# Attention and Fourier mixing on one core: sequence matrices first, one of them by two levels of seven products, the output projection in two parts

## The chip, the core and the metric

The program runs on one core of a Trainium2 chip. The metric is the device time of one execution in microseconds (us); lower is better. The time before is the median of three runs. An engine name stands for one of the core's engines: PE is TensorE (matrix products; PEld is its weight load), DVE is VectorE, ACT is ScalarE, POOL is GpSimd, and SP is SyncE, which here only issues DMA transfers.

## The reference

Two independent blocks on inputs of 2048 rows and 1024 columns; their results stand side by side in the output (2048 x 2048).

```python
# A: softmax attention with 32 heads of 32
q, k, v = split_heads(x @ wqkv)                       # 1024 x 3072
p = softmax(einsum("bhqd,bhkd->bhqk", q, k) * Dh**-0.5)
a = concat_heads(einsum("bhqk,bhkd->bhqd", p, v)) @ wo
# B: real part of a two-dimensional Fourier transform by matrices
re = einsum("bsd,ed->bse", x, dft_hid_re)             # 1024 x 1024
im = einsum("bsd,ed->bse", x, dft_hid_im)
b = einsum("ts,bse->bte", dft_seq_re, re) - einsum("ts,bse->bte", dft_seq_im, im)
out = concatenate([a, b], axis=-1)
```

## The kernel before

**Products.** Every large product runs in single precision as three passes. `halves` splits each operand into a rounded high half `hi` (a cast, on DVE or ACT) and the rest `lo` (a subtraction of two SBUF tiles, on POOL or DVE), and `group` adds hi·hi, lo·hi and hi·lo into one PSUM bank. One such pass is one PE instruction: a stationary tile of 128x128 and a moving tile of 128x512. The text calls it a *fill*, since these instructions fill the gaps that attention leaves on PE. `piece` makes a stationary operand ("h" and "l" tiles, from rings of four), `moving` makes a moving one (a numbered "slot" that holds both halves). `fetch` loads the one or two terms of an operand (tiles "raw" and "g") and adds or subtracts them on POOL or DVE.

**Seven products for eight.** Each matrix product is cut into two by two blocks and done with seven block products (`ORDER` = 1, 2, 5, 6, 7, 3, 4). Operands are sums of blocks, some reused through DRAM (`s_d`, `t_d`), and `gather` combines the results, one DVE instruction that reads PSUM ("evacuation") per group, sometimes with a further addition on POOL or DVE.

**Stages.** `qkv` makes queries, keys and values (2016 fills). `dense1` multiplies x by the two hidden matrices (7 block products x 8 row tiles x 2 matrices x 4 chunks x 3 passes = 1344 fills) and stores the results (`ab_d`). `dense2` does the two sequence matrices one after the other (2 x 7 x 8 x 8 x 3 = 2688 fills) and adds them through `y_d`. `project` multiplies the attention output, read back from `o_d`, by `wo` (7 x 8 x 4 x 3 = 672 fills). In sum 6720.

**Attention.** Per head, 64 score products and 64 transposed score products of 128x512, and 16 times four products with the values; DVE takes row maxima, ACT the exponentials. The streams S, T and V hold these.

**Order.** Nothing is scheduled at run time. `Plan` walks through the program when it is built, keeps a clock with a fixed cost for each operation, and writes one order for each engine; on the chip every engine works through its own order and waits on semaphores. The fills are one list, in the order of the code. Between them the loop puts attention so that the share of fills done keeps pace with the share of attention done (`nf / (FILL - RES) <= done / ATT`); what is then left of the list runs after the last head. `Plan` does not let POOL start while a DVE instruction that uses both SBUF ports (`two=True`) runs, nor the other way round (`choose`). It counts a DMA by its size alone, at `KB_US` = 360 KB per us.

Of the kernel before, what the change touches and what calls it, by code (L numbers as in the profile page):

```python
# [8 lines left out]
F32 = mybir.dt.float32  # L9
F32R = mybir.dt.float32r  # L10
AF = mybir.ActivationFunctionType
ALU = mybir.AluOpType
# [208 lines left out]
def kernel(  # L221
# [26 lines left out]
    ab_d = [[[dram.tile([P, NB], F32, name=f"ab_d{m}_{e}_{k}") for k in range(NS)] for e in range(2)] for m in range(2)]  # L248

    s1_d = [[dram.tile([P, 4, P], F32, name=f"s1_d{x}_{i}") for i in range(8)] for x in (5, 6)]  # L250
    t1_d = [[dram.tile([P, NB], F32, name=f"t1_d{x}_{n}") for n in range(8)] for x in (5, 6)]
# [5 lines left out]
    u3_d = [[dram.tile([P, NB], F32, name=f"u3_d{i}_{m}") for m in range(2)] for i in range(8)]  # L257
    s2_d = [[[dram.tile([P, 4, P], F32, name=f"s2_d{x}_{i}_{k}") for k in range(4)] for i in range(8)] for x in (5, 6)]
    t2_d = [[[dram.tile([P, NB], F32, name=f"t2_d{x}_{m}_{k}") for k in range(8)] for m in range(2)] for x in (5, 6)]
    y_d = [[dram.tile([P, NB], F32, name=f"y_d{i}_{e}") for e in range(2)] for i in range(NS)]  # L260
# [83 lines left out]

    MM, PV, SWITCH, TINY = 0.2275, 0.853, 0.40, 0.17
# [8 lines left out]
    RES = 400  # L354
# [7 lines left out]
    FILL = 3 * (7 * 24 * 4 + 7 * 16 * 4 + 7 * 8 * 16 + 2 * 8 * 4)  # L362
# [251 lines left out]
    def qkv():  # L614
# [216 lines left out]
        def qk_group(x, W, b, n, order=None):  # L831
# [3 lines left out]
            if p == 1 and n == 0:  # L835
                if early:
                    X[2 * b], X[2 * b + 1] = acc(b)
                else:
# [3 lines left out]
                  gather(p, 2 * b + n, qk_result(b + 8 * h[0], 2 * h[1] + n, early) if h else None, early, None if b % 2 else SCALE), order)  # L842

# [7 lines left out]
        for x, (p, blocks, v) in enumerate(STEPS[:10]):  # L851
            spare[0] = x < 5
# [69 lines left out]
    ORDER = (1, 2, 5, 6, 7, 3, 4)  # L922

# [7 lines left out]
    def gather(what, X, Y, u3, to, wrote, part=None, split=False):  # L931
# [14 lines left out]
        def finish(ps, last):  # L946
# [48 lines left out]

            if what == 1:
                return to_acc(X, None, True)
# [12 lines left out]
            if what in (2, 3):  # L1010
                return put(X.at, [X.users], X.last, ALU.add, to, wrote, part)
            if Y is None:
                return put(lambda: got["c"], [cusers], cload, ALU.subtract, to, wrote, part)
            return put(Y.at, [Y.users], Y.last, ALU.subtract, to, wrote, part)
# [3 lines left out]
    ab_st = [[[[] for _ in range(NS)] for _ in range(2)] for _ in range(2)]  # L1018

    def dense1():  # L1020
        s1, t1 = ({5: [[] for _ in range(8)], 6: [[] for _ in range(8)]} for _ in range(2))
        u3 = [[[], []] for _ in range(8)]

        def a_terms(p, i):
            q = lambda r, k: xb[8 * r + i, :, 4 * k : 4 * k + 4, :]
            return {
                1: [(1, q(0, 0), [])], 2: [(1, q(0, 1), [])], 4: [(1, q(1, 1), [])],
                5: [(1, q(1, 0), []), (1, q(1, 1), [])],
                6: [(1, s1_d[0][i], s1[5][i]), (-1, q(0, 0), [])],
                7: [(1, q(0, 0), []), (-1, q(1, 0), [])],  # L1030
                3: [(1, q(0, 1), []), (-1, s1_d[1][i], s1[6][i])],
            }[p]

        def b_terms(p, n):
            m, c = divmod(n, 4)
            q = lambda k, e: wd[m, 4 * k + c, :, e * NB : e * NB + NB]
            return {
                1: [(1, q(0, 0), [])], 2: [(1, q(1, 0), [])], 3: [(1, q(1, 1), [])],
                5: [(1, q(0, 1), []), (-1, q(0, 0), [])],
                6: [(1, q(1, 1), []), (-1, t1_d[0][n], t1[5][n])],  # L1040
                7: [(1, q(1, 1), []), (-1, q(0, 1), [])],
                4: [(1, t1_d[1][n], t1[6][n]), (-1, q(1, 0), [])],
            }[p]

        def load_b(x, n):
            p = ORDER[x]
            B[x][n] = moving((8 * x + n) % 12, b_terms(p, n), (t1_d[p - 5][n], t1[p][n]) if p in (5, 6) else None)

# [542 lines left out]
```

## Time and profile before

| What | Value |
|---|---|
| Median of 3 runs | 2942.08 us (2942.07 to 2944.09) |
| Span of the profiled execution | 2940.5 us (1.6 us under the median; the page gives no time of its own around the span) |
| PE busy, instructions | 2934.3 us (100%), 14920 |
| DVE, ACT, POOL busy | 79%, 77%, 28% |
| Granted PE clock | 1.000 |
| DMA | 562.78 MB, 191 GB/s over the span, 58.8% of 16 engines on the SP queue |

Fills run alone at first; the first score products stand at 69 us, from about 240 us attention and fills share PE, and the last products with the values end at about 2760 us, after which fills run alone again. The windows view splits the span into stretches and gives for each the busy time and the number of instructions of each engine, the mean share of the 16 DMA engines that was busy, and the rate.

### The profile page before, as it was taken

Reading aid. Unit: us, or ns where it says so; the run is one execution under the profiler, and the core shown is the slowest. Engines: PE = TensorE matmul, PEld = TensorE weight load, DVE = VectorE, ACT = ScalarE, POOL = GpSimd, SP = SyncE. Lnnn points to the kernel's source line nnn. Section 1 sums busy time; section 2 is a strip of 40 time slices with the busy share of each in tenths; the row PEclk is TensorE's granted clock in tenths of the full one; section 3 lists DMA queues with packets and bytes.
Section 4 is the critical chain, followed back from the end, with each engine's and each line's share of the span. In section 5 each row is a group of like instructions: output and inputs, shape, how many; then the busy total and the mean of one; then the engine's idle time right before and its main releaser. Section 6 shows DMA issues by size and latency. Waiting matters only on the chain.

```text
span 2940.5 us, 45511 instructions
## 1 busy us (share of the span) xinstructions
PE 2934.3 (100%) x14920; PEld 2146.0 (73%) x14920; DVE 2328.2 (79%) x3196; ACT 2278.3 (77%) x4317; POOL 833.3 (28%) x650
## 2 busy tenths in 40 slices
PE   9999999999999999999999999999999999999999
PEld 8887777777777767777777777777777777677787
DVE  7679888788877987777777898888777888887585
ACT  5347888888888888888888888888888888887431
POOL 2324335132212332241111332333112333343042
PEclk9999999999999999999999999999999999999999
DMA  9965668676525653664425775554334677555663
GB/s 372 348 229 194 195 191 292 194 251 225 191 93 164 226 189 111 205 206 147 150 84 161 237 224 189 171 167 151 110 110 139 220 238 222 168 178 176 211 209 118
DMA packets 378455, 562.78 MB, mean 191 GB/s; under 512 B 111183, under 2 KB 111439, under 8 KB 378095
## 3 DMA queue, kind: packets, MB, share of 16 engines
q1 hardware_dynamic: 378076, 559.75, 58.8%
q8 instruction: 120, 1.97, 0.3%
q14 instruction: 115, 0.93, 0.1%
q10 hardware_dynamic: 144, 0.13, 0.0%
HBM read 385.65 MB, written 174.08 MB: 190 GB/s over the span
## 4 chain that ended last, share of the span: by engine, by line
PE 98%; DMA 1%; DVE 1%; ACT 0%; issue 0%; POOL 0%; SPq 0%; DVEq 0%; POOLq 0%; ACTq 0%
PE pd L404 44%; PE psT L1400 16%; PE psS L1278 16%; PE pd L1419 15%; PE psT L404 7%; DVE negm L1284 0%; DMA raw<-in_xb 0%; DMA g<-in_ct 0%; DMA raw<-ab_d 0%; ACT psS L1287 0%; DMA g<-in_xb 0%; DMA slot<-in_xw 0%; DVE l L494 0%; POOL raw L469 0%; DVE raw L469 0%
## 5 line engine op out<-in xcount | busy, mean ns | idle before, releaser
L1404 ACT ACTIVATE pt<-psT 128x512 f32<-128x512 f32 x2048 | 1193.8, 671 | 347.3 <-PE psT L1400 345.5
L1284 DVE TENSOR_REDUCE negm<-psS 128x1 f32<-128x1024 f32 x1024 | 1241.2, 1220 | 211.5 <-PE psS L1278 204.4
L1287 ACT ACTIVATE psS<-psS,negm 128x1024 f32<-128x1024 f32 x1024 | 1188.9, 1161 | 70.9 <-DVE negm L1284 66.8
L404 PE MATMUL pd<-slot,h 128*128 128x512 f32 x3400 | 1155.7, 389 | 0.0
L1400 PE MATMUL psT<-qs,ks 128*128 128x512 f32 x2048 | 802.3, 395 | 0.0
L404 PEld LDWEIGHTS pd<-slot,h 128*128 128x128 f32 x3400 | 638.3, 188 | 132.6
L404 PE MATMUL pd<-slot,l 128*128 128x512 f32 x1700 | 661.3, 389 | 0.0
L1400 PEld LDWEIGHTS psT<-qs,ks 128*128 128x128 f32 x2048 | 381.4, 188 | 157.3 <-issue 63.7
L1278 PE MATMUL psS<-ks,qs 128*128 128x512 f32 x1552 | 472.1, 390 | 0.7 <-ACT psS L1287 0.6
L1419 PE MATMUL pd<-pt,vt 128*32 128x512 f32 x4096 | 459.3, 594 | 0.0
L494 POOL TENSOR_TENSOR l<-raw,h 128x512 fp32r<-128x512 f32 x143 | 184.7, 1292 | 707.8 <-PE psT L1400 366.5
L404 PEld LDWEIGHTS pd<-slot,l 128*128 128x128 f32 x1700 | 319.1, 188 | 67.3 <-issue 0.8
L494 POOL TENSOR_TENSOR slot<-raw,slot 128x512 fp32r<-128x512 f32 x162 | 208.4, 1291 | 535.5 <-DVE slot L491 197.6
L469 POOL TENSOR_TENSOR raw<-raw,g 128x512 f32<-128x512 f32 x186 | 241.9, 1306 | 397.4 <-DMA raw<-t_d 48.9
L1278 PEld LDWEIGHTS psS<-ks,qs 128*128 128x128 f32 x1552 | 290.7, 188 | 62.2 <-ACT psS L1287 3.3
L1419 PEld LDWEIGHTS pd<-pt,vt 128*32 128x32 f32 x4096 | 123.3, 110 | 282.6 <-issue 265.7
L1287 ACT ACTIVATION_READ_ACCUMULATOR psS<-psS,negm 128x1 f32 x1024 | 285.9, 279 | 0.0
L404 PE MATMUL pd<-slot,slot 128*128 128x512 f32 x768 | 191.9, 389 | 0.0
L1432 DVE TENSOR_TENSOR ot<-ot,pd 128x512 f32<-128x512 f32 x64 | 44.0, 687 | 155.1 <-PE pd L1419 154.9
L404 PEld LDWEIGHTS pd<-slot,slot 128*128 128x128 f32 x768 | 144.2, 188 | 30.0
L491 DVE CAST h<-raw 128x512 fp32r<-128x512 f32 x321 | 147.5, 461 | 17.4 <-PE pd L404 14.2
L1278 PE MATMUL psS<-ks,qx 128*128 128x512 f32 x496 | 149.1, 391 | 0.0
(130 smaller groups left out, 1858.4 us busy)
## 6 DMA issues: line engine op xcount, KB each, us to landing
raw<-in_ct SPq DMA_DIRECT2D x192, 256.0 KB
qk_d<-e SPq DMA_DIRECT2D x52, 512.0 KB
qs<-qk_d SPq DMA_DIRECT2D x128, 192.0 KB
ks<-qk_d SPq DMA_DIRECT2D x128, 192.0 KB
raw<-ab_d SPq DMA_DIRECT2D x96, 256.0 KB
g<-in_ct SPq DMA_DIRECT2D x96, 256.0 KB
c<-u_d SPq DMA_DIRECT2D x88, 256.0 KB
s_d<-raw SPq DMA_DIRECT2D x80, 256.0 KB
```

Source lines behind the costliest of these rows:

```text
L404: nc.tensor.matmul(box["ps"], a[1]((a[0].hi, a[0].lo)[u]()), b[1]((b[0].hi, b[0].lo)[v]()), start=k == 0, stop=k == n - 1)
L469: (nc.gpsimd if e == "POOL" else nc.vector).tensor_tensor(out=dest(), in0=dest() if a is None else a.get(), in1=other["q"] if "q" in other ...
L491: nc.vector.tensor_copy(hi(), raw())
L494: (nc.gpsimd if e == "POOL" else nc.vector).tensor_tensor(out=lo(), in0=raw(), in1=f(hi()), op=ALU.subtract)
L1278: nc.tensor.matmul(p[:, i * NB : i * NB + NB], (QX[0] if own else QS[h % 2])[:, qt * P : qt * P + P], KS[h % 2][:, c * 1024 + i * NB : c * ...
L1284: nc.vector.tensor_reduce(out=ST["negm"][:, c, qt : qt + 1], in_=box["p"], axis=AX.X, op=ALU.max, negate=True)
L1287: nc.scalar.activation(box["p"], box["p"], AF.Exp, bias=ST["negm"][:, c, qt : qt + 1], accum_out=ST["sums"][:, c, qt : qt + 1])
L1400: nc.tensor.matmul(box["p"], KS[h % 2][:, t * P : t * P + P], QS[h % 2][:, j * NB : j * NB + NB], start=True, stop=True)
L1404: nc.scalar.activation(box["t"], box["p"], AF.Exp)
L1419: nc.tensor.matmul(po["p"][j * DH : j * DH + DH, :], VT[h][:, k, :], box["t"], start=(k == t0), stop=(k == t), tile_position=(0, j * DH),)
L1432: nc.vector.tensor_tensor(out=po["o"], in0=po["o"], in1=po["p"], op=ALU.add)
```

## The change

The order of the Fourier block is turned round. `dense1` now multiplies the transposed input by the two sequence matrices (cosine, r = 0, and sine, r = 1), and `dense2` multiplies the result `g_d` by the hidden matrices, both in one sum. For r = 0 each of the seven block products is done plainly ("one-level part", 7 x 8 groups x 8 chunks x 3 = 1344 fills). For r = 1 (`TWO`) each is again cut into seven ("two-level part", 7 x 7 x 2 groups x 4 chunks x 3 = 1176 fills). `dense2` is 7 x 8 x 8 x 3 = 1344 fills. The projection of heads 0 to 23 (`project(1)`: 7 x 8 x 3 x 3 = 504) stands behind the first block product of `dense2`, its result goes to `py_d`, and heads 24 to 31 (`project_end`: 16 x 2 x 2 x 3 = 192) come last and are added to it. In sum 6576 fills.

"Made ahead" means that the stationary pieces of the two-level part are split during the one-level part and kept in DRAM as both halves (`ha_d`, by `keep_a` and `aside_c`); `again` loads them. 30 sums of blocks of the sine matrix are made during `qkv` (`aside`, into `tg_d`). In the two-level part the sixteen moving tiles of a block product stay in SBUF (`R`), and `load_b` adds and splits them there, tile "slot" from "slot". `gather1` and `gather2` keep running sums in DRAM (`xo_d`, `yo_d`). `spare[0] = True` lets ACT take casts in all stages.

```diff
-    RES = 400
+    RES = 700
-    FILL = 3 * (7 * 24 * 4 + 7 * 16 * 4 + 7 * 8 * 16 + 2 * 8 * 4)
+    FILL = 3 * (7 * 24 * 4 + sum(7 * 2 * 4 if (r, q) in TWO else 8 * 8 for r in range(2) for q in ORDER) + 7 * 8 * 8 +  7 * 8 * 3)
+    TWO = {(1,q) for q in ORDER}
...
-            spare[0] = x < 5
+            spare[0] = True
...
+            if 5 <= x < 8:
+                aside((12, 13, 14))
...
+    def keep_a(a, pp, p, i):
+        rank = seq()
+        kept_a[pp, p, i] = [op("SP", ISSUE, lambda k=k, t=t: nc.sync.dma_start(ha_d[pp][p][i][:, k * NB : k * NB + NB], f(t()).rearrange("p t c -> p (t c)")), [made], [u], rank, 256)
+                            for k, (t, made, u) in enumerate(zip((a.hi, a.lo), a.made, a.users.lists))]
...
+        def load_b(o, x, kk):
...
+            r = lambda k, n: R[(2 * k + n) * 4 + kk]
+            terms, keep = {
+                1: ([(1, r(0, 0))], None), 2: ([(1, r(1, 0))], None), 3: ([(1, r(1, 1))], None),
+                5: ([(1, r(0, 1)), (-1, r(0, 0))], r(0, 0)), 6: ([(1, r(1, 1)), (-1, r(0, 0))], r(0, 0)),
+                7: ([(1, r(1, 1)), (-1, r(0, 1))], r(0, 1)), 4: ([(1, r(0, 0)), (-1, r(1, 0))], r(1, 0)),
+            }[p]
+            M[o, x, kk] = moving((4 * (7 * o + x) + kk + 8) % 10, terms, None, keep)
...
+        def again(pp, p, i):
...
+            for k, (key, ring) in enumerate(zip("hl", (HR, LR))):
+                d, st = ha_d[pp][p][i][:, k * NB : k * NB + NB], kept_a[pp, p, i][k % len(kept_a[pp, p, i])]
...
+                made.append(op("SP", ISSUE, lambda d=d, get=get: nc.sync.dma_start(f(get()).rearrange("p t c -> p (t c)"), d), old + [st], [users], rank, 256, ring))
...
+        for o, (r, pp) in enumerate(outers):
...
+                    to = g_d[r][hh[0]][nt][:, :, c, :].rearrange("t p c -> p t c")
...
+            if (r, pp) not in TWO:
+                for n in range(2):
+                    for m in range(4):
...
+                                if (pp, key, i) in kept_a:
+                                    a = again(pp, key, i)
+                                else:
+                                    a = piece([a_outer(pp, m, k)])
+                                    keep_a(a, pp, key, i)
...
+                        group(terms(), 8, gather1(pp, *place_of((r1, n), i), XY[1][pos] if r in PURE else None, XY[5][pos] if r in PURE and pp in (5, 7, 4) else None))
...
+                        aside_c()
+                continue
+            for x, p in enumerate(ORDER):
...
+                for i in range(2):
+                    a = again(pp, p, i) if (pp, p, i) in kept_a else a_piece(pp, p, i)
+                    group(((chunk(a, c), (M[o, x, c], whole)) for c in range(4)), 4, gather2(pp, p, X[i], Y[i] if p not in (1, 2) else None, *place_of(QUAD.get(p), i)))
...
-    behind()
-    project()
+    project_end()
```

**SP, the middle of the first stage of the Fourier block.** The rows name the destination, then the source. Before, this is the hidden product, with loads of x (`in_xb`), partial results (`u3_d`, printed as u_d) and stores of `ab_d`:

```order
L942 DMA c<-u_d_1_412 128x512
L990 DMA u_d_1_410<-c 128x512
L453 DMA raw<-in_xb 128x512
L942 DMA c<-u_d_0_397 128x512
L453 DMA raw<-in_xb 128x512
L982 DMA ab_d_1_15_232<-e 128x512
L453 DMA raw<-t_d_1_290 128x512
L990 DMA u_d_0_411<-c 128x512
L462 DMA g<-s_d_4_277 128x512
```

Now it is the one-level part. Two terms of the sine and cosine matrices (`in_ct`) for a moving tile, sums stored to `tg_d`, halves loaded back from `ha_d` as "h" and "l", and other halves stored to `ha_d` for later:

```order
L461 DMA raw<-in_ct 128x512
L486 DMA tg_d_0_13_450<-raw 128x512
L1594 DMA h<-ha_d_1_1_348 128x512
L1594 DMA l<-ha_d_1_1_348 128x512
L470 DMA g<-in_ct 128x512
L1594 DMA h<-ha_d_2_1_350 128x512
L486 DMA tg_d_0_14_451<-raw 128x512
L1594 DMA l<-ha_d_2_1_350 128x512
L461 DMA raw<-in_ct 128x512
L1298 DMA ha_d_7_0_343<-c 128x512
```

A stationary piece that is loaded as halves takes two transfers where a plain one takes one, and the stores of halves for the later part stand among the loads.

**POOL, the sequence matrices.** Before, in `dense2`, POOL adds terms (raw, g) and makes low halves ("l", "slot"), with a combination of results (`e`) between:

```order
L494 TENSOR_TENSOR slot_20664<-raw,slot_20664 128x512
L992 TENSOR_TENSOR slot_18544<-e,slot_18544 128x512
L469 TENSOR_TENSOR raw<-raw,g 128x512
L494 TENSOR_TENSOR l<-raw,h 128x512 x2
L469 TENSOR_TENSOR raw<-raw,g 128x512
```

Now, in the two-level part, sums and low halves of the resident tiles (L477 and L502) follow one another, with the outer combinations of `gather2` (L1056) between:

```order
L502 TENSOR_TENSOR slot_20090<-slot_15518,slot_20090 128x512
L502 TENSOR_TENSOR slot_20098<-slot_15518,slot_20098 128x512
L477 TENSOR_TENSOR slot_15655<-slot_17043,slot_15655 128x512
L1056 TENSOR_TENSOR e<-c,e 128x512
L477 TENSOR_TENSOR slot_16562<-slot_15518,slot_16562 128x512
L502 TENSOR_TENSOR slot_20178<-slot_15655,slot_20178 128x512
L1056 TENSOR_TENSOR e<-c,e 128x512
```

The stationary halves no longer pass through POOL here; they come from `ha_d`.

**PE, the last products.** Before, the last group of the projection is four times three fills:

```order
L404 MATMUL psT<-slot_31355,slot_31447 128x512 x3
L404 MATMUL psT<-slot_31366,slot_31453 128x512 x3
L404 MATMUL psT<-slot_31374,slot_31459 128x512 x3
L404 MATMUL psT<-slot_31384,slot_31466 128x512 x3
```

Now the last three groups of `project_end` are:

```order
L412 MATMUL psT<-slot_32672,slot_32830 128x512 x3
L412 MATMUL psT<-slot_32716,slot_32872 128x512 x3
L412 MATMUL psT<-slot_32706,slot_32830 128x512 x3
L412 MATMUL psT<-slot_32743,slot_32872 128x512 x3
L412 MATMUL pd<-slot_32706,slot_32830 128x512 x3
L412 MATMUL pd<-slot_32743,slot_32872 128x512 x3
```

Each group is now six fills, and each is followed by an output store.

More of the change, by code (lines that the diff above doesn't have):

```diff
@@ L1133, in op_pool @@
+            if x == 0:
+                project(1)
+                for k in range(4):
+                    X[1, k] = accs(16 + k)
+                    for n, acc in enumerate(X[1, k]):
+                        acc.last = op("SP", ISSUE, lambda acc=acc, i=2 * k + n: nc.sync.dma_start(acc.at(), x1_d[i]), [*acc.old, *x1[2 * k + n]], [acc.users], seq() - 4, 256)
     def op_pool():
```

767 lines of the change are left out of this document (580 added, 187 removed).

## The prediction

> **What bounds the kernel now.** I read the page's busy times first, then what TensorE (PE) waited for, then the windows. Of the page:
>
> ```profile
> PE 2934.3 (100%) x14920; PEld 2146.0 (73%) x14920; DVE 2328.2 (79%) x3196; ACT 2278.3 (77%) x4317; POOL 833.3 (28%) x650
> PEclk9999999999999999999999999999999999999999
> DMA  9965668676525653664425775554334677555663
> DMA packets 378455, 562.78 MB, mean 191 GB/s; under 512 B 111183, under 2 KB 111439, under 8 KB 378095
> PE 98%; DMA 1%; DVE 1%; ACT 0%; issue 0%; POOL 0%; SPq 0%; DVEq 0%; POOLq 0%; ACTq 0%
> ```
>
> The last line is the chain that ended last: PE is 98% of it. PE's own waits, as the waits view gives them:
>
> ```profile
> PE pd L369 <- DVE c L367: 1.5, 1, 1.5
> PE psS L1278 <- ACT psS L1287: 0.6, 3, 0.2
> PE psT L404 <- ACT slot L489: 0.2, 1, 0.2
> ```
>
> Together 2.3 us, 1.5 of them at the start. The ends of products are modelled, so "100% busy" alone proves little; the counts in the windows prove more. Columns: stretch, length, busy us and number of instructions of PE, PEld, DVE, ACT, POOL, clock, share of the DMA engines, GB/s.
>
> ```profile
> 40.00:50.00 10.00, 10.00 (x46) 8.29 (x45) 8.85 (x14) 6.11 (x11) 2.10 (x2) 1.00 1.06 406
> 100.00:200.00 100.00, 100.00 (x443) 82.81 (x442) 69.16 (x97) 34.41 (x57) 22.02 (x17) 1.00 0.82 294
> 774.00:1459.00 685.00, 684.66 (x3559) 489.52 (x3558) 534.59 (x710) 582.50 (x1114) 160.60 (x125) 1.00 0.52 165
> 2100.00:2200.00 100.00, 100.00 (x525) 71.38 (x524) 76.52 (x103) 85.58 (x165) 11.60 (x9) 1.00 0.34 103
> 2300.00:2400.00 100.00, 100.00 (x507) 73.70 (x503) 84.16 (x115) 86.10 (x165) 46.36 (x37) 1.00 0.80 262
> 2800.00:2900.00 100.00, 100.00 (x443) 82.79 (x442) 87.46 (x121) 32.31 (x55) 46.97 (x36) 1.00 0.52 175
> 2900.00:2941.00 41.00, 36.63 (x162) 30.01 (x160) 12.32 (x18) 2.53 (x4) 1.41 (x2) 0.99 0.25 97
> ```
>
> Two stretches with hardly anything but fills, 2700 us apart, both hold 443 products in 100 us: 0.2257 us each, at full clock. The stretch 40 to 50 holds 46 in 10 us, the same rate, although the DMA engines are full there (share 1.06). So PE bounds the kernel from the first us to the last 4.4, and a fill less is worth 0.2257 us as long as its operands come in time.
>
> **What the change removes: products.** In the built order PE has 12874 matrix instructions before and 12730 after; attention is the same, so 144 fills are gone (6720 to 6576: the sine matrix loses 168, the projection gains 24). 144 x 0.2257 = 32.5 us. Nothing else stands on PE's path before, so the whole of it counts, unless something comes late. 156 fills leave the attention stretch (`FILL - RES` goes from 5840 to 5684) and 12 more run after it; both kinds are priced alike.
>
> **What it adds on the other engines.** Prices from the groups (count, busy us and mean ns):
>
> ```profile
> L469 POOL TENSOR_TENSOR raw<-raw,g 128x512 f32<-128x512 f32 x186 | 241.9, 1306 | 397.4 <-DMA raw<-t_d 48.9 <-issue 47.5 <-DVE l L494 39.8
> L469 DVE TENSOR_TENSOR raw<-raw,g 128x512 f32<-128x512 f32 x122 | 87.5, 726 | 16.2 <-DMA raw<-ab_d 5.1 <-DMA raw<-s_d 4.7 <-DMA g<-in_ct 2.6
> L491 DVE CAST h<-raw 128x512 fp32r<-128x512 f32 x321 | 147.5, 461 | 17.4 <-PE pd L404 14.2 <-issue 0.9 <-DMA raw<-in_wqk 0.7
> L489 ACT ACTIVATE slot<-raw 128x512 fp32r<-128x512 f32 x58 | 35.6, 630 | 82.6 <-PE psT L404 34.8 <-DVE raw L469 15.6 <-DMA raw<-in_wo 15.4
> ```
>
> In the built order DVE gets 53 instructions more (3198 to 3251), ACT 170 (3296 to 3466, all casts), POOL 233 (655 to 888). ACT: 170 x 0.63 = 107 us over some 2500 us, 4 points on 86%; POOL: 233 x 1.306 = 304 us on 833. I price both at nothing: the rows 2100 to 2400 leave 14 us of ACT and over 50 us of POOL idle in each 100. If ACT's cover went, each cast in front of an exponential would cost PE its 0.63 us, 107 us at the very most; POOL's case is a rival below.
>
> **What it adds on the DMA queue.** SP issues 3192 transfers instead of 2445 (rows of equal transfers counted singly); nearly all of the 747 are of 256 KB, so some 196 MB more, 759 in all. They are not spread evenly. I placed each on an axis of PE's work: every product of 128x512 by 0.2257 us, the products with the values by 0.853 us a step (eight instructions), all stretched by 1.021 so that the order of before fills 2940.5 us. The 0.853 is the code's `PV`; in the timeline of PE the last six steps bear it out, with one modelled end in the 5.36 us:
>
> ```profile
> 2755.12 5.36 PE L1419 MATMUL pd<-pt,vt 128*32 128x512 f32 x48
> ```
>
> For the old `dense1` this gives 112.3 MB in 685 us, 164 GB/s; the row 774:1459 measured 165, so the counting holds. For the one-level part, also 1344 fills, it gives 936 transfers and 220 MB in 681 us, 322 GB/s, with 256-KB transfers of halves (`ha_d`) as the main addition (315 of the 936). By block product:
>
> | block product | 1 | 2 | 5 | 6 | 7 | 3 | 4 |
> |---|---|---|---|---|---|---|---|
> | us on PE | 97 | 95 | 98 | 100 | 94 | 98 | 100 |
> | GB/s needed | 258 | 301 | 317 | 380 | 355 | 344 | 300 |
>
> What can the engines carry beside attention? From 103 GB/s at share 0.34 to 262 at 0.80 the rows rise by 346 GB/s per whole share. Products 6, 7 and 3 need 104.9 MB in 291 us, 360 GB/s: share 0.80 + (360 - 262) / 346 = 1.083. In this part also lie 15 stores of `g_d` with pieces of 512 bytes. The trace has no transfer of such pieces, so I bound it by the packets that it has. At 406 / 1.06 = 383 GB/s per whole share (row 40:50) a 2-KB packet takes one engine 2048 x 16 / 383 = 86 ns. The row of the queue says that all packets took 58.8% of 2940.5 us, 1729 us; 560 MB at 383 GB/s are 1461 us, and the 268 us left are 268 x 16 / 111183 = 39 ns for each of the small packets. The 512 pieces of a store then take 0.55 us more than its 0.7 at the small packet's price, 2.1 us more at the large one's, and nothing more if only bytes count. I take 0.8, nearer to the small packets.
>
> ```profile
> q1 hardware_dynamic: 378076, 559.75, 58.8%
> ```
>
> So 1.083 + 15 x 0.8 / 291 = 1.124. The highest share in any row is 1.06 (40:50). Then 291 us of products need 291 x 1.124 / 1.06 = 309 us of transfers: 18 us late. Some 3 us of that are covered by tiles that are already there when the stretch begins; I take **15 us**. The ends: 0, if the 406 GB/s of the row hold (104.9 MB in 258 us); and 61, if all five products from 5 to 4 (490 us, 166.2 MB, 339 GB/s, 24 such stores) run at share 1.00 with stores at the full price: 490 x 1.023 + 24 x 2.1 = 551. What is behind a late tile: PE takes its list in order, so the score products behind a fill wait too, then the maxima on DVE and the exponentials on ACT; SP is also in order, so a store of halves that waits for its cast holds back the loads behind it.
>
> The Trainium skill, page "DMA: Bandwidth & Descriptors", section "Where 436 GB/s comes from", puts the limit for HBM traffic of one core at about 358 GB/s. By that figure the 104.9 MB would take 293 us, an estimate, and 2 us would be lost instead of 15 (2913.6 us). The row 40:50 with 406 GB/s does not agree with it as a ceiling, and the figure counts bytes alone.
>
> The rest of the change: 30 sums made ahead in `qkv` (90 transfers, 24 MB) raise its mean by the same count from 221 to 265 GB/s, share 0.81: no cost, up to 5 us in a burst. **The end:** 32 groups of six fills, 1.36 us each, with a 256-KB store behind each, and 32 loads of `py_d`: 64 transfers of 0.7 us in 43 us of products. The evacuation is 0.69 us of 1.36. The last stores can queue; before, 4.4 us pass without PE at the end (row 2900:2941). I add 2 us (0 to 6). The wait of the projection for heads 0 to 23 costs nothing: it stands behind 4728 of 5684 fills, where by the pace 26.6 heads are done.
>
> **Sum,** against the profiled execution: 2940.5 - 32.5 + 15 + 2 = 2925.0 us of span; the median of the runs lies 1.6 us over the span, so 2926.6 us.
>
> **Rivals.**
>
> *All hidden.* The DMA engines carry 380 GB/s in bursts, as in 40:50, and PE never waits. For it: PE held its rate there. Against it: that stretch has no attention, whose small packets take time, and lasts about 140 us, not 290. 2940.5 - 32.5 + 1.6 = 2909.6 us.
>
> *Slower: the one-level part is bound by its transfers.* Share 1.00 is the end, 512-byte pieces cost as 2-KB ones, and the lag is 61 us instead of 15. For it: the part as a whole needs a share of 0.80 + (322 - 262) / 346 = 0.97 and has no slack to catch up. Against it: the shares over 1.00 at the start. 2940.5 - 32.5 + 61 + 2 + 1.6 = 2972.6 us. It decides from a lag of 36 us on, that is, if products 6, 7 and 3 move less than 104.9 MB in 327 us, 321 GB/s.
>
> *POOL and DVE in the two-level part.* 309 POOL instructions by 1.29 us (399 us) and 272 of DVE on SBUF tiles alone, 0.46 to 0.73 us, some 155 us: 554 of 590 us if they exclude each other, as the planner's `choose` has it. A tenth more time for each makes 609, 19 us too many: 2926.6 + 19 = 2945.6 us, no change. Against it: in 2800:2900 POOL is busy 47 us and DVE 87, by the order some 40 of them on SBUF tiles alone, so 87 of 100 us are taken, and PE loses nothing. The Trainium skill, page "SBUF — State Buffer", section "Who interferes with whom", says why they may exclude each other: VectorE with two SBUF inputs and GpSimd hold a shared port pair for the whole instruction. By that rule alone 554 us still fit into 590, and the time would be the forecast's; the 87 us of the row agree with it, but do not prove it.
>
> **How the numbers follow.** Forecast 0.45, all hidden 0.20, transfers bind 0.20, POOL and DVE 0.15. That fewer products are issued at all is counted, so it is no rival. A measurement of this kernel tells about 0.2%, 6 us, from no change. Faster by more (under 2936.2): 0.43 of the forecast, all of the hidden case and 0.03 of the last, 0.66. Slower by more (over 2948): most of the third, 0.19, and 0.04 of the last, 0.23. Same: 0.11. The range reaches from a little under the hidden case, 2906, to 2960, which leaves out the upper half of the third case (0.10) and small ends elsewhere.
>
> **What would show it.** In the profile after: PE instructions 144 fewer, clock 1.00. In the one-level part, about 760 to 1440 us, DMA digits of 9 and shares over 1.0, and there alone waits of PE's fills for transfers ("DMA h<-ha_d", "raw<-in_ct") of some 15 us; all hidden shows none. POOL at 6 or 7 tenths in the two-level part, without waits of PE for it. If PE waits there for POOL or DVE, or if the one-level part falls under 321 GB/s with 36 us of waits, the forecast is wrong.

## The result, and the profile after

| | before | after |
|---|---|---|
| Median | 2942.77 us (4 runs) | 2958.70 us (4 runs, 2956.75 to 2965.21) |
| Ratio to before, 95% interval | | 1.0057 (1.0043 to 1.0071) |
| Span of the profiled execution | 2940.5 us | 2958.1 us |
| Granted PE clock | 1.000 | 0.997 |

The kernel became slower by 0.6%; the forecast was 2926.6 us, faster. The spans differ by 17.6 us, and 144 fills are gone, which are worth 32.5 us. So 17.6 + 32.5 = 50.1 us were lost somewhere in the new kernel. The page of after, in the order in which the page of before was shown:

```profile
PE 2924.5 (99%) x14776; PEld 2120.4 (72%) x14776; DVE 2378.0 (80%) x3249; ACT 2370.3 (80%) x4487; POOL 1124.1 (38%) x883
DMA  9979968667879999999988778886556555775468
DMA packets 510614, 758.78 MB, mean 257 GB/s; under 512 B 123134, under 2 KB 156158, under 8 KB 510238
q1 hardware_dynamic: 510220, 755.61, 77.9%
PE 85%; DMA 9%; DVE 3%; ACT 1%; SPq 1%; issue 1%; POOL 1%; DVEq 0%; POOLq 0%; ACTq 0%
```

PE has exactly 144 instructions fewer, and the bytes are the 759 MB that were counted. But the chain that ended last is PE for 85% instead of 98%: it now runs through transfers. PE's waits in after (in all, times, longest):

```profile
PE psS L1786 <- ACT psS L1795: 9.2, 12, 2.3
PE psT L1908 <- DMA qs<-m_d: 4.3, 3, 2.2
PE psT L1908 <- ACT pt L1912: 3.7, 4, 1.2
PE pd L412 <- DVE e L682: 3.0, 1, 3.0
PE pd L412 <- DMA l<-ha_d: 2.7, 2, 2.1
PE pd L412 <- POOL l L502: 2.5, 1, 2.5
PE pd L377 <- DVE c L375: 1.5, 1, 1.5
PE psS L1786 <- DMA ks<-qk_d: 1.3, 1, 1.3
```

Some 29 us instead of 2.3, in many small pieces and for all sorts of releasers. No single one is the cause. These 27 us more and 10 us of lost clock (below) are 37 of the 50 us; the views do not tell what the other 13 were. Three stretches, first of before, then of after (columns as in the prediction):

```profile
1000.00:1500.00 500.00, 499.84 (x2598) 357.79 (x2597) 389.10 (x519) 426.06 (x817) 117.11 (x91) 1.00 0.51 160
200.00:400.00 200.00, 200.00 (x1010) 147.89 (x1008) 168.07 (x228) 161.44 (x305) 75.02 (x58) 1.00 0.59 184
1500.00:2000.00 500.00, 499.77 (x2603) 358.12 (x2602) 411.62 (x566) 424.67 (x814) 150.15 (x117) 1.00 0.59 185
```

```profile
1000.00:1500.00 500.00, 486.94 (x2474) 338.95 (x2473) 413.86 (x558) 429.90 (x816) 198.35 (x155) 0.99 0.97 327
200.00:400.00 200.00, 192.26 (x922) 140.33 (x921) 157.21 (x200) 159.92 (x300) 91.53 (x71) 0.98 0.89 295
1500.00:2000.00 500.00, 495.50 (x2563) 352.99 (x2562) 437.31 (x605) 435.97 (x836) 321.13 (x254) 0.99 0.81 261
```

In 200 to 400 us, where the 30 sums are made ahead, PE issues 922 instructions instead of 1010; in 1000 to 1500, most of the one-level part, 2474 instead of 2598. The clock is below 1.00 in both. What the waits look like from behind, in the chain of waits between 1090 and 1290 us (start, length, what):

```profile
1159.81 4.72 DMA ha_d<-c
1164.59 4.79 DMA c<-so_d
1221.77 4.70 DMA m_d<-lt
1226.53 4.38 DMA qs<-m_d
1254.82 5.48 DMA ha_d<-c
```

A store of a made-ahead piece holds the tile "c" for 5 us, and the load into that tile takes 5 more; `m_d` and `qs`, two transfers of 16 KB that gate score products, take 9 us together, each from issue to landing.

`Plan` does not count a transfer by its size alone: it reckons 0.7 us for 256 KB, 1.6 us (`LANDING`) for any transfer to land, and up to 1.0 us (`QUEUE`) behind the transfers in front, so 2.3 to 3.3 us from issue to landing. A reader on PE, DVE or POOL gets 2.0 us more (`SLACK`), so it stands 4.3 to 5.3 us behind the issue; a reader on ACT, and a load into a tile that a store has to leave, get nothing more. `LANDING` moves all of these. Over all transfers whose landing ended a wait of some engine between 1000 and 1500 us, the median from issue to landing, worked out from the traces, is 3.6 us in before (83 transfers) and 5.3 us in after (380). By the median, then, before had room for its readers, and after has none.

A table of loss serves for the experiments below. The total is the span minus 2940.5 us, plus 0.2257 us for each fill fewer than 6720 (less for each one more). A stretch's loss is its length less the price of the products that PE starts in it by the trace (0.2257 us each, 0.853 / 8 us for a product with the values), less what the same sum gives for before; so each row adds up to its total, up to rounding. A profiled run can lie some us from the median of its kernel: e9 by 7 and e3, e13 and e16 by 3 us under it, e15 by 2 over it.

| us lost in | total | 200–400 | 400–600 | 1000–1500 | 1500–1800 | 1800–2100 | elsewhere |
|---|---|---|---|---|---|---|---|
| after | 50 | 14 | 2 | 23 | -1 | 8 | 4 |
| e1, no sums ahead | 55 | 0 | 4 | 26 | 13 | 5 | 8 |
| e2, no pieces ahead | 60 | 13 | 1 | 2 | 17 | 20 | 6 |
| e3, one level only | 9 | 0 | 3 | 4 | 1 | 0 | 2 |
| e5, pieces without arithmetic | 52 | 14 | 2 | 15 | 0 | 11 | 11 |
| e6, sums later | 44 | 1 | 13 | 25 | 1 | 3 | 2 |
| e7, split again | 48 | 14 | 1 | 17 | 4 | 10 | 2 |
| e9, both | 42 | 1 | 9 | 14 | 5 | 10 | 4 |
| e10, both, landing 2.4 | 56 | 2 | 9 | 2 | 31 | 7 | 4 |
| e12, before with more stores | 10 | 0 | 0 | 8 | 2 | 0 | 0 |
| e13, after, landing 2.4 | 26 | 5 | 4 | 6 | 0 | 9 | 2 |
| e15, both edits, landing 2.4 | 30 | 4 | 4 | 9 | 4 | 7 | 2 |
| e16, as e12, landing 2.4 | 20 | 1 | 6 | 2 | 0 | 1 | 9 |
| e17, as e13, landing 1.6 | 59 | 14 | 1 | 26 | 1 | 12 | 5 |

### The profile page after: what moved, and what is told of

It is laid out like the page before. It is cut to its first block, busy times and chain, and to the rows that moved or that the text cites. A ratio compares the mean times of both kernels' runs of the same rounds, so it can differ in the third digit from the quotient of the medians.

```text
span 2958.1 us, 47210 instructions
## 1 busy us (share of the span) xinstructions
PE 2924.5 (99%) x14776; PEld 2120.4 (72%) x14776; DVE 2378.0 (80%) x3249; ACT 2370.3 (80%) x4487; POOL 1124.1 (38%) x883
## 2 busy tenths in 40 slices
DMA packets 510614, 758.78 MB, mean 257 GB/s; under 512 B 123134, under 2 KB 156158, under 8 KB 510238
## 3 DMA queue, kind: packets, MB, share of 16 engines
q1 hardware_dynamic: 510220, 755.61, 77.9%
q14 instruction: 130, 1.06, 0.1%
## 4 chain that ended last, share of the span: by engine, by line
PE 85%; DMA 9%; DVE 3%; ACT 1%; SPq 1%; issue 1%; POOL 1%; DVEq 0%; POOLq 0%; ACTq 0%
PE pd L412 39%; PE psT L1908 14%; PE psS L1786 13%; PE pd L1927 13%; PE psT L412 5%; DMA ha_d<-c 2%; DVE negm L1792 1%; DMA g<-in_ct 1%; DMA raw<-in_ct 1%; ACT psS L1795 1%; DMA slot<-tg_d 0%; DMA h<-ha_d 0%; DMA tg_d<-slot 0%; DMA l<-ha_d 0%; DMA qs<-m_d 0%
## 5 line engine op out<-in xcount | busy, mean ns | idle before, releaser
L502 POOL TENSOR_TENSOR slot<-raw,slot 128x512 fp32r<-128x512 f32 x151 | 193.7, 1290 | 434.5 <-DVE slot L499 100.3
L477 POOL TENSOR_TENSOR raw<-raw,g 128x512 f32<-128x512 f32 x143 | 184.9, 1296 | 358.7 <-DVE negm L1792 49.8
L1795 ACT ACTIVATION_READ_ACCUMULATOR psS<-psS,negm 128x1 f32 x1024 | 279.7, 273 | 0.0
L502 POOL TENSOR_TENSOR l<-raw,h 128x512 fp32r<-128x512 f32 x110 | 141.9, 1290 | 293.0 <-PE psT L1908 69.2
L502 POOL TENSOR_TENSOR slot<-slot,slot 128x512 fp32r<-128x512 f32 x149 | 190.2, 1292 | 139.6 <-DVE slot L502 29.6
L412 PE MATMUL pd<-slot,slot 128*128 128x512 f32 x780 | 212.0, 390 | 0.2 <-DVE e L734 0.2
L477 DVE TENSOR_TENSOR raw<-raw,g 128x512 f32<-128x512 f32 x133 | 100.9, 763 | 27.0 <-issue 7.1
```

The lines of the kernel that those rows point to most:

```text
L412: nc.tensor.matmul(box["ps"], a[1]((a[0].hi, a[0].lo)[u]()), b[1]((b[0].hi, b[0].lo)[v]()), start=k == 0, stop=k == n - 1)
L477: (nc.gpsimd if e == "POOL" else nc.vector).tensor_tensor(out=dest(), in0=dest() if a is None else a.get(), in1=other["q"] if "q" in other ...
L502: (nc.gpsimd if e == "POOL" else nc.vector).tensor_tensor(out=lo(), in0=raw(), in1=f(hi()), op=ALU.subtract)
L1795: nc.scalar.activation(box["p"], box["p"], AF.Exp, bias=ST["negm"][:, c, qt : qt + 1], accum_out=ST["sums"][:, c, qt : qt + 1])
```

## The experiments

**Where it is lost.** e1 makes the sums not ahead, but where they are used; e2 does the same with the pieces of `aside_c`; e3 leaves out the second level (6744 fills).

```diff
e1, e3  -            if 5 <= x < 8:
        +            if x < 0:
e2      -                        if r == 0 and (1, pp) in TWO:
        +                        if r < 0:
e3      -    TWO = {(1,q) for q in ORDER}
        +    TWO = set()
```

> The changed kernel without the 30 sums of the sine matrix that are made ahead during qkv; the two-level part then loads two terms for each instead. In its profile the changed kernel lost some 16 us in the stretch 200 to 400 us. Theory A (transfers queue up where the sums are made ahead, and everything behind them comes late): that loss goes, PE has no waits over 1 us before 400 us; the two-level part gets 24 MB more and may lose 0 to 8 us of it again: 2943 to 2951 us. Rival B (the loss in 200 to 400 is from the casts that ACT now takes): it stays, 2956 to 2966 us.

> The changed kernel without the stationary pieces made ahead in the one-level part: 56 pieces are split in the two-level part itself. The one-level part loses some 170 of its 936 transfers (to about 30 MB per 100 us), and POOL in the two-level part rises to about 80 of 100 us. Theory A (the one-level part is late by its transfers): its waits, some 27 us with what follows from them, fall to under 8 us; the two-level part pays 0 to 10 us: 2936 to 2950 us. Rival C (POOL and DVE bind in the two-level part): the gain is eaten there, waits of PE for POOL or DVE of more than 15 us between 1400 and 2000 us, 2955 us or more.

> The turned order and the split projection alone: both sequence matrices plainly, nothing made ahead, 6744 fills (168 more than the changed kernel, 24 more than before). Counting fills alone gives 2943 + 5 = 2948 us. Theory A: transfers stay near 30 MB per 100 us at most, few waits: 2946 to 2954 us. Rival D (the turned order or the split projection itself costs time): over 2958 us.

Measured: e1 2965.43 us, 1.0080 (1.0065 to 1.0095); e2 2968.32, 1.0086 (1.0071 to 1.0101); e3 2960.45, 1.0060 (1.0045 to 1.0075). First e1, then e2:

```profile
200.00:400.00 200.00, 200.00 (x1003) 149.59 (x1005) 161.49 (x214) 170.48 (x322) 76.53 (x59) 1.00 0.59 183
1500.00:2000.00 500.00, 491.54 (x2514) 345.25 (x2516) 435.68 (x578) 444.44 (x852) 348.77 (x275) 1.00 0.86 280
```

```profile
1000.00:1500.00 500.00, 498.09 (x2586) 356.05 (x2579) 396.40 (x524) 435.57 (x835) 188.47 (x148) 1.00 0.85 277
1500.00:2000.00 500.00, 485.18 (x2463) 332.00 (x2463) 439.80 (x597) 448.32 (x861) 349.34 (x276) 0.99 0.83 267
```

Each edit clears its own stretch almost wholly (200 to 400 in e1, 1000 to 1500 in e2) and both times later stretches lose it again: between 1500 and 2100 us e1 loses 18 us and e2 37, where after loses 7. So the sums cost 14 us and the one-level part is late because of the pieces made in it, but neither is better done elsewhere. e3 loses only 9 us beside its 24 fills more than before (12 by the medians): nearly all of the loss belongs to the second level.

**Transfers or engines.** e5 keeps the transfers of `aside_c` and leaves out its arithmetic; e7 loads the raw piece again and splits it in place of loading both halves; e12 takes the kernel before and adds only stores.

```diff
e5      -        made = op("POOL", SUB, ...)     # and the cast "high", and "low" but one column
e7      -                                if (pp, key, i) in kept_a:
        -                                    a = again(pp, key, i)
        -                                else:
        -                                    a = piece([a_outer(pp, m, k)])
        -                                    keep_a(a, pp, key, i)
        +                                a = piece([a_outer(pp, m, k)])
        +                                if n == 0 and key:
        +                                    keep_a(a, pp, key, i)
e12     +                    for c in range(4):
        +                        t = B[x][4 * m + c]
        +                        op("SP", ISSUE, lambda t=t, n=...: nc.sync.dma_start(dm_d[n], t.hi().bitcast(F32)), [frees[-4], *t.made], [t.users], seq(), 256)
```

> The pieces for products 6, 7 and 3 are loaded and stored as in the changed kernel, with the same bytes, but their 84 operations of arithmetic (sum, high half, low half) are left out except for one column each, so the sine part of the output is not the reference's. Theory A, the transfers: the one-level part is late because its transfers fill the queues; the loss between 1000 and 1500 us stays above 20 us (27 in the changed kernel), DMA share stays at 0.95 or more there, and the time stays at 2953 to 2960. Theory B, the engines that work in order: the pieces' operations wait for their loads on DVE and POOL and hold the maxima and sums of the attention behind them; then the loss there falls below 10 us, though the bytes are the same, and the time goes to 2935 to 2945.

> In the one-level part the second use of a piece loads the raw piece and splits it again, instead of loading its two halves: 84 transfers of 256 KB fewer (22 MB), for 61 more subtractions on POOL and about as many on DVE and ACT. Theory A, the transfers: the loss of 27 us between 1000 and 1500 falls below 14, DMA share there goes from 0.97 to about 0.90, and the time goes to 2940 to 2948. Theory B, the engines in order: more work on POOL and DVE makes the part no earlier, the loss stays above 22 us or grows, and the time is 2955 to 2965.

> The kernel before, with 448 more stores of 256 KB in its hidden product, four behind each group of fills: moving tiles that are in SBUF anyway are written to DRAM that nobody reads. No arithmetic is added and nobody waits for these stores, but the hidden product then moves about 34 MB per 100 us, as the one-level part does after the change. Theory A, bytes alone make the part late: 15 to 30 us are lost between 700 and 1450 us and the time is 2955 to 2975. Theory B, the change's losses come from its chains (sum, cast, store, load again) and its order on the engines: fewer than 6 us, 2942 to 2949.

Measured: e5 2961.40 us, 1.0064 (1.0047 to 1.0081); e7 2956.66, 1.0050 (1.0035 to 1.0065); e12 2952.38, 1.0033 (1.0018 to 1.0047). The stretch 800 to 1500 of after, then of e5:

```profile
800.00:1500.00 700.00, 685.33 (x3493) 481.54 (x3492) 574.39 (x775) 604.37 (x1149) 262.49 (x205) 1.00 0.94 313
```

```profile
800.00:1500.00 700.00, 684.47 (x3507) 484.53 (x3506) 539.05 (x717) 589.37 (x1126) 213.90 (x208) 1.00 0.95 318
```

Without the arithmetic PE gets 14 instructions further in 700 us, 4 us by their prices; about half of what e5 loses less after 1000 us it loses more before, and its total is no smaller. So it is not the arithmetic of these pieces on POOL, DVE and ACT. e7, with 22 MB less, clears 6 of the 23 us between 1000 and 1500 us; the 17 left lie between the bounds of its two theories, and its median falls by 2 us only, since more is lost elsewhere. And e12 moves as many bytes in that part as the changed kernel. Before, then e12:

```profile
700.00:1450.00 750.00, 749.66 (x3889) 537.41 (x3888) 593.21 (x798) 638.81 (x1223) 178.57 (x140) 1.00 0.54 174
```

```profile
700.00:1450.00 750.00, 744.30 (x3857) 530.42 (x3856) 588.58 (x790) 633.50 (x1212) 174.50 (x137) 1.00 0.94 326
```

It loses 7 us there and 10 in all, less than theory A's 15 and more than theory B's 6. Under the plan of before, then, a queue as full as this costs the old order a third of the 23 us.

**The plan.** What is left is when the readers stand in each engine's list. e4 was the first try, with a plan that reckons transfers slower in both terms; e10 raises only `LANDING`, on top of the two edits of e6 and e7.

```diff
e4       -    KB_US = 360.0
         -    LANDING = 1.6
         +    KB_US = 320.0
         +    LANDING = 3.2
e10      -    LANDING = 1.6
         +    LANDING = 2.4
```

> The changed kernel with a planner that reckons 320 KB per us instead of 360 and 3.2 us from the end of a transfer's share to its landing instead of 1.6; the same instructions in another order. Theory A1 (the bytes fit, the plan only starts consumers too early): PE's waits fall from 27 us over before to under 12 and the time to 2930 to 2945 us. Theory A2 (the DMA engines are simply full): the lost time moves, but stays, 2952 to 2965 us.

> As the kernel with both edits, and the plan reckons 2.4 us from a transfer's issue to its landing instead of 1.6 (besides its size at 360 KB per us), so operations that need a load stand later in the orders. The instructions are the same but for the engine of some. If losses come from operations that the plan puts too early behind transfers that land in 4 to 6 us, the PE waits for DMA and ACT shrink by half and the time falls by 5 to 10 us against that kernel. If the queue is full, a later place of the readers makes nothing land sooner: within 4 us of it.

Measured: e4 3046.93 us, 1.0350 (1.0333 to 1.0367); e10 2964.33, 1.0073 (1.0058 to 1.0088). Both miss, for one reason. First e4, then e10:

```profile
1700.00:1800.00 100.00, 66.66 (x217) 33.32 (x221) 69.10 (x96) 59.78 (x109) 19.31 (x16) 0.66 0.47 144
```

```profile
1600.00:1700.00 100.00, 85.21 (x352) 52.03 (x354) 78.62 (x108) 74.55 (x139) 38.80 (x31) 0.80 0.63 201
1000.00:1500.00 500.00, 499.30 (x2568) 357.92 (x2567) 444.44 (x613) 446.48 (x856) 255.42 (x200) 1.00 0.91 302
```

In these 100 us the order has a long row of attention without a fill between (81 us in e4, 49 us in e10); PE waits in short steps and the clock halves. In e10 that hole takes 31 us, but the stretch 1000 to 1500 us, 14 us late with the same edits in e9, is only 2 us late. e13 to e17 take the hole away and part the two. Of the last block product (4) only half of the pieces is made ahead, in e13 with `LANDING` 2.4 and in e17 with 1.6; both are otherwise the changed kernel. e14 is e10 with that half, and e16 is e12 with 2.4.

```diff
e13, e14, e17  -                        if r == 0 and (1, pp) in TWO:
               +                        if r == 0 and (1, pp) in TWO and (pp != 4 or m == 2):
e13, e14, e16  -    LANDING = 1.6
               +    LANDING = 2.4
```

> The changed kernel with the same work, but its plan reckons 2.4 us from a transfer's issue to its landing instead of 1.6; and of the last block product only half of the pieces is made ahead (without that, a late plan leaves 30 to 57 us with attention alone at the start of the two-level part, as two kernels showed). 754 MB instead of 756. If the loss is made by the plan, that orders readers before transfers that land in 4 to 6 us, it shrinks from 54 to 30 us or less, in the one-level part from 27 to below 12, and the time is 2930 to 2942. If the queue's rate alone makes it, it stays: 2952 to 2962.

> The changed kernel with its plan as it was (1.6 us), but of the last block product only half of the pieces is made ahead: the other of the two edits in the kernel planned at 2.4 us, by itself. If the plan's landing time made the 20 us, this stays at 2954 to 2962. If the four pieces less did, it comes to 2936 to 2945.

> Both edits (sums later, second splitting) and the plan at 2.4 us, as the kernel that lost 30 us in one gap of its order, but with half of the last product's pieces not made ahead, so that the order has no such gap. Without the gap that kernel's own profile leaves 2963.5 - 30 = 2933 us of span: 2930 to 2940. If what was not lost elsewhere in it was only made up for during the gap, 2950 to 2960.

> The kernel before with the 448 further stores, which lost 10 us, now planned at 2.4 us of landing. If those 10 us came of readers that the plan puts too early, most of them go: 2941 to 2946. If they came of the rate of the queue, they stay: 2950 to 2955.

Measured: e13 2938.79 us, 0.9987 (0.9977 to 0.9996); e17 2968.87, 1.0092 (1.0075 to 1.0108); e14 2939.98, 0.9989 (0.9980 to 0.9998); e16 2965.05, 1.0075 (1.0060 to 1.0090). e17, then e13:

```profile
1000.00:1500.00 500.00, 482.32 (x2461) 337.81 (x2460) 412.10 (x556) 425.94 (x809) 195.37 (x153) 0.99 0.96 322
200.00:400.00 200.00, 191.89 (x922) 140.13 (x921) 158.71 (x200) 160.10 (x300) 91.98 (x71) 0.98 0.89 295
```

```profile
1000.00:1500.00 500.00, 497.20 (x2568) 351.87 (x2561) 424.26 (x580) 437.99 (x836) 205.06 (x161) 1.00 0.97 327
200.00:400.00 200.00, 197.87 (x963) 146.24 (x962) 170.88 (x222) 170.31 (x322) 91.64 (x71) 1.00 0.86 296
```

Same work (but for the engine of some additions and casts), same share of the queue, nearly the same rate, and PE issues 107 instructions more in 500 us. The number in the plan is worth 30 us of median. The hole was the pieces' part: e14 loses nothing in 1600 to 1700, where e10 lost 31 us. The pieces alone gain nothing: e17 is 10 us slower than the changed kernel. The transfers of e13 still take as long (the median of above is 5.1 us in e17 and in e13): in its chain between 1090 and 1290 us stand

```profile
1152.43 4.85 DMA ha_d<-c
1157.29 5.88 DMA c<-so_d
1243.14 6.46 DMA raw<-in_xb
```

but other engines wait for them, at other places. In e17 SP, which issues in order, waits long for stores to leave "c", and DVE waits for the pieces' sums:

```profile
SPq L1289 <- DMA ha_d<-c: 71.1, 40, 4.0
DVE c L1295 <- DMA c<-so_d: 15.0, 12, 2.8
```

In e13 both shrink, and POOL takes 32 of these 52 sums instead of 25. It waits there for 59.5 us instead of 27.5, and among PE's waits in e13 none is for POOL:

```profile
SPq L1289 <- DMA ha_d<-c: 38.3, 29, 2.6
DVE c L1295 <- DMA c<-so_d: 3.7, 4, 2.3
POOL c L1295 <- DMA c<-so_d: 59.5, 10, 22.8
```

That the landing time does it is shown by the pair; that it does so through these two waits, and not through the sums that change their engine or another reader, is read from the rows and not tried singly. Three pairs differ in this number alone, and in each the loss in the full stretch falls: between 1000 and 1500 us from 26 us to 6 (e17, e13) and from 14 to 2 (e9, e10), and between 700 and 1450 us from 7 to 3 (e12, e16). e16 there:

```profile
700.00:1450.00 750.00, 746.59 (x3874) 534.14 (x3873) 580.59 (x786) 632.44 (x1210) 188.70 (x147) 1.00 0.94 328
```

e16 shows the limit too: its median is 13 us over that of e12. Of the 20 us that its profile lost, 17 lie outside of that stretch, where e12 lost 3: 6 between 400 and 600 us and 8 after 2500 us. So a later landing time helps where the queue is full and can cost more than that elsewhere; by which waits it costs there stays open.

**The clock.** In after, a wait of 3.0 us ends at 271 us:

```profile
265.00:270.00 5.00, 2.96 (x11) 1.61 (x9) 2.07 (x3) 4.48 (x9) 2.51 (x2) 1.00 1.00 370
270.00:275.00 5.00, 4.01 (x12) 3.23 (x13) 3.80 (x5) 3.47 (x6) 1.28 (x1) 0.73 1.05 390
275.00:280.00 5.00, 5.00 (x21) 4.04 (x21) 3.38 (x4) 4.11 (x9) 1.29 (x1) 0.93 1.02 370
```

After this wait, not in it, PE runs at half clock for a while. e8 repeats a POOL subtraction at six places of the kernel before, to make waits of known origin.

```diff
+            for _ in range({130: 4, 160: 6, 190: 8, 215: 10, 240: 12, 270: 14}.get(lows[0], 1) if e == "POOL" else 1):
```

> The kernel before, with one subtraction on POOL repeated 4, 6, 8, 10, 12 and 14 times at six places in it, so that TensorE has to wait there for some us. If a wait of 1.8 us or more halves the clock for about 3.3 us afterwards, each of the longer waits is followed by fills at 0.43 us instead of 0.2257 and costs about 1.5 us beyond itself, and waits below 1.5 us cost nothing beyond themselves. If what follows long waits in the changed kernel is only the next late buffer, the fills after these waits run at 0.2257 us throughout.

Measured: 2969.04 us, 1.0090 (1.0070 to 1.0110). The waits of PE in it, and the stretches around the second and third:

```profile
PE psS L1280 <- ACT psS L1289: 9.7, 4, 7.9
PE pd L404 <- POOL slot L496: 3.7, 1, 3.7
PE psT L1402 <- DMA qs<-m_d: 3.3, 1, 3.3
PE pd L404 <- DVE ot L1432: 1.4, 1, 1.4
```

```profile
1665.00:1670.00 5.00, 2.92 (x11) 1.23 (x15) 1.37 (x2) 0.00 (x0) 4.92 (x5) 0.59 0.31 96
1680.00:1685.00 5.00, 5.00 (x17) 3.94 (x16) 4.05 (x6) 3.10 (x6) 2.40 (x2) 0.71 0.97 315
```

In a kernel whose clock had not fallen before its last product, the long waits (for ACT, POOL and a transfer) come with half clock, and the wait of 1.4 us does not: a wait causes it, whatever was waited for. In windows of 1 us each such stretch lacks 1.70 or 1.71 us of clock, that is 3.4 us at half, or twice that. After has six of them, 10 of its 50 us.

**Toward a better kernel.** e6 starts the sums two steps later and lets their loads wait for the group in front; e9 has this and the edit of e7; e11 is e9 with only four products cut twice. e15 and e18 are e14 with the sums one step earlier, e18 at 2.0 us.

```diff
e6, e9, e10, e11, e14  -            if 5 <= x < 8:
                       +            if 7 <= x < 10:
e15, e18               +            if 6 <= x < 9:
all of these           -... src), old + t[2], [users], rank, 256) for j, t in enumerate(terms)]
                       +... src), old + t[2] + [frees[-1]], [users], rank, 256) for j, t in enumerate(terms)]
e11                    +    TWO = {(1,q) for q in (1, 2, 3, 4)}
e18                    +    LANDING = 2.0
```

> The 30 sums made ahead start two steps later, and their loads wait for the group of matmuls in front of them, so that the order has 21 MB instead of 34 between 200 and 300 us, and 37 instead of 29 between 400 and 500. If the loss of 16 us between 200 and 400 comes of too many transfers at once, it falls by half or more there, and the time goes to 2944 to 2952, with no more than 4 us of it coming back between 400 and 600. If the sums' place is of no matter, only that POOL and SP take them in order, the loss moves with them and the time stays at 2955 to 2962.

> The later start of the 30 sums and the second splitting of pieces in the one-level part together: 84 transfers fewer than the changed kernel and 21 MB instead of 34 between 200 and 300 us. Each alone gave 4 and 2 us. If each loss is local to the stretch whose transfers come late, the two add up, with the 12 us that the second splitting saved in the one-level part showing now: 2944 to 2951. If what is saved in one stretch is lost in the next, since the two-level part has no slack either: 2952 to 2957.

> As the kernel with both edits, but only four of the seven block products of the sine matrix (1, 2, 3, 4) are cut a second time: 72 fills more (16.3 us), 24 transfers fewer. If the second level costs in proportion to its products, its losses fall with them and the time stays within 4 us of that kernel. If a few of its products are free and the rest cost, it is faster, 2940 to 2947. If the losses come of the turned order and not of the second level, it is slower by about 16 us.

> As that kernel, with the 30 sums one step earlier, so that they spread over 200 to 500 us (27, 32 and 32 MB in each 100 us instead of 21, 29 and 36). If the 7 us lost between 400 and 500 come of the burst there, it is faster by 2 to 5 us; if any place costs the same, within 2 us.

> Both edits with the sums one step earlier, and the plan at 2.0 us instead of 2.4. If the best landing time lies nearer to what transfers take (4 to 6 us in the full stretches), 2.0 is worse than 2.4: 2940 to 2950. If most of the gain is had by a little more room, it is as good or better, 2932 to 2939, because the quiet stretches are delayed less.

| | median us | ratio to before |
|---|---|---|
| e6 | 2954.29 | 1.0040 (1.0025 to 1.0055) |
| e9 | 2959.12 | 1.0053 (1.0037 to 1.0069) |
| e11 | 2955.64 | 1.0045 (1.0030 to 1.0060) |
| e15 | 2937.72 | 0.9978 (0.9969 to 0.9988) |
| e18 | 2940.39 | 0.9995 (0.9986 to 1.0004) |

e6 moves 14 us out of 200 to 400, and 11 of them come back in 400 to 600. The two edits together do not add up under the old plan (e9). In e11 the 72 fills more (16.3 us) are paid by about as much less loss. With the plan at 2.4 us the same edits end under before, e15 by 0.22%, the best of this study, though only 1 us under e13; its loss is still 30 us, near that of e13. Most of the gain is had at 2.0 us (e18).

## Why the prediction was wrong, step by step

- **The fills.** Right: 144 fewer, and no other instruction of PE. The bytes were right too: 759 MB, and for the part from 760 to 1445 us the forecast was 220 MB at 322 GB/s:

```profile
DMA packets 146914, 215.36 MB, mean 314 GB/s; under 512 B 32572, under 2 KB 46908, under 8 KB 146822
```

- **The one-level part, 15 us.** It was 23 in 1000 to 1500 us. The step that failed is that lateness was worked out from the share of the engines that the bytes need (1.124 over 1.06), with no term for an order built for quick landings. At the same 327 GB/s and 0.97, e13 loses 6; at 326 GB/s e12 loses 7. So the rate explains the smaller part of the 23 at most; the larger goes with a later landing in the plan alone (26 us in e17, 6 in e13): a transfer under this load lands in about 5 us, and the order has been written for landings after 2.3 to 3.3 and readers after 4.3 to 5.3. The queue did not go to the share that the forecast counted with: no 100 us of that part have one over 0.99. Nor did PE wait where the forecast put it: between 760 and 1440 us its fills wait 1.1 us, 0.6 of them for `ha_d`, and its score products 12 us, for ACT and for `qs`. The prediction named the waiters behind a late tile and SP's order, but gave them no price of their own. So that 15 came near 23 was luck. Nor is it the rival "bound by its transfers": that needs 36 us and under 321 GB/s.
- **The 30 sums, "no cost, up to 5 us in a burst".** It was 14, all of it gone in e1. A mean share of 0.81 was taken for a cover; in the burst the row 265:270 has 1.00, and a fill waits 3.0 us there for an evacuation.
- **ACT, DVE and POOL, nothing.** Nearly right for the pieces of the one-level part (4 us in e5). The two-level part lost 7 us net in 1500 to 2100, against 0 in the forecast and 19 in the rival; PE's waits there are 2.3 us for ACT and 2.1 us for `ha_d`, none for POOL or DVE.
- **The small packets, 39 ns.** By the queue's row of after, 0.779 x 2958.1 = 2304 us; 755.61 MB at 383 GB/s are 1973; the 331 left make 331 x 16 / 156158 = 34 ns. So the estimate held roughly with the new 512-byte pieces among them.
- **The end, 2 us.** Between 0 and 2: after 2100 us after loses 2 in all.
- **The clock, 1.00.** It was 0.997. The forecast had no term for it: 10 us.
- **The figure of the Trainium skill,** page "DMA: Bandwidth & Descriptors": its limit of 358 GB/s would have meant 2 us of loss instead of 15. Neither was the mechanism. Its section "Latency and other measured facts" says that an access to HBM takes 0.2 us on average and 2 us under high load; the medians of 3.6 us in before and 5.3 us in after agree in direction, and the prediction made no use of it.

So the sum missed 33 us of span (2925.0 against 2958.1): 8 in the one-level part, 14 in the sums, 7 in the two-level part and 4 elsewhere; the clock's 10 us lie within these.

## What to carry to other kernels

An order that is fixed when the kernel is built carries the latencies that it was built with. A change that fills the transfer queue changes these latencies, so its forecast needs a term for every reader placed by the old ones, even where the queue keeps up; and one number in the planner (here 0.8 us of landing, 30 us of time) is the first thing to try again after such a change, and to measure, since the same 0.8 us made another order 13 us slower. Where PE is the bound, a wait of some 2 us costs nearly twice its length.

## What the runs showed of the hardware that was not expected

- Half clock after short waits. Over the runs of this study without long holes, 22 of 24 waits of PE of 2.0 us and more brought 1.7 us (or twice that) of missing clock, which began within 1.4 us of their end or, in some of the longer ones, still in them; of those between 1.4 and 1.6 us none did, and of those between 1.6 and 1.9 us about half. The Trainium skill, page "TensorE: Matmul & The Clock Gate", part 1 on the clock gate, gives a free-running window of about 3.4 us and half the clock after an idle one. The length of the dips agrees with that window; that a whole window must be idle does not, since a wait of 1.8 us was enough. Nor need it be one wait: four such stretches follow two shorter waits of 1.7 to 1.85 us together within 3.4 us (in e13 0.6 and 1.1 us, before 2026 us).
- A transfer queue at a share of 0.97 for 500 us (e13) beside a PE that loses 6 us, about 1%: that transfers take 5 us costs little by itself.
